# One 128-partition output store in place of two 64-partition stores, in a fused attention and MLP kernel

## The chip, the cores and the metric

The kernel runs on one core of a Trainium2 chip. The time is the device time of one execution in microseconds (us). Before the change it was 218.69 us, the median of 3 runs (217.29 to 221.75).

Engines, as the profile abbreviates them: PE is the matmul engine, PEld its weight loads, DVE VectorE, ACT ScalarE, POOL GpSimd, SP SyncE. "SPq" is SP's sequencer, which issues nearly all transfers, one after the other in the timelines below (its queue carries 96576 of the 96742 packets of the kernel before); the moving is done by DMA engines, of which the page counts 16. L404 is a line of that kernel's file; a changed kernel has its lines moved by one or two.

## The reference, cut to what matters

```python
# q, k, v: (4, 8, 768, 64) float32; lam: (8,); w_in: (512, 2048); w_out: (2048, 512)
for each block of 64 tokens:          # causal attention with decay, state carried over blocks
    out = (q k^T * Dmask) v + (q * lam_pow) kv_state
    kv_state = lam^64 * kv_state + (k * rev_pow)^T v
x = attention output as (3072 tokens, 512)
h = x @ w_in;  g = h * sigmoid(1.702 h);  out = g @ w_out      # (3072, 512) float32
```

## The kernel before

The kernel works in six waves of 512 tokens. Waves 0 and 1 take 256 tokens each of two sequences, waves 2 to 5 take 128 tokens each of all four. In waves 0 and 1 two neighbouring tokens share a partition when they are loaded. Their output columns therefore come out in the order (j, m), where the token is 2m + j: first the 64 even tokens of a tile, then the 64 odd ones. A tile of 128 tokens by 512 float32 (256 KB) was stored like this:

```python
def store(w, g, o, cols=slice(0, d_model)):
    if w < 2:
        r0 = (2 * w + g // 2) * S + (g % 2) * P
        dst = out[r0 : r0 + P, cols].rearrange("(m j) d -> j m d", j=2)
        for j in range(2):
            nc.sync.dma_start(out=dst[j], in_=o[hd(j), :])     # 64 partitions, every second row
    else:
        r0 = g * S + w * P
        nc.sync.dma_start(out=out[r0 : r0 + P, cols], in_=o)   # 128 partitions, consecutive rows
```

The same SP queue carries what the matmuls of the later waves need: the loads of k, q and v, and two kinds of transposing transfers.

```python
def p_cast(w, p):                       # waves 2 to 5, p = 0 to 3
    ...                                 # VectorE writes kqs from the loaded k and q
    nc.sync.dma_start_transpose(out=kq_of[w, p]..., in_=kqs...)   # PE's scores wait for this

def p_out(w, p):
    ...
    nc.scalar.copy(xs.rearrange("s b h d -> s h b d"), o)
    nc.sync.dma_start_transpose(out=xT(w)[:, p], in_=xs...)       # xs has two buffers

def u_x(w, bl, p):                      # waves 0 and 1: ScalarE writes xT itself
    nc.scalar.copy(xT(w)[:, p, 2 * bl : 2 * bl + 2, :], uo_ps.pop((w, bl, p))[:, :, 0:P])
```

## Time and profile before

| | kernel before |
|---|---|
| time, median of 3 runs | 218.69 us (217.29 to 221.75) |
| profiled execution | span 220.2 us (this execution took 221.89 us, slower than the three above) |
| PE busy | 209.7 us, 95% |
| PE's part of the chain that ended last | 81% |
| transfers under way, first half | 9 tenths of the DMA engines' time in most slices |

From the profile page of the kernel before. The first line gives the busy us, the share of the span and the instruction count of PE. The next three cut the span into 40 slices of 5.5 us: PE's granted clock in tenths, the busy share of the DMA engines in tenths, and the GB/s that they moved. The last is the queue that SP issues on: its packets, MB, and share of 16 engines' time.

```profile
PE 209.7 (95%) x1769; PEld 108.9 (49%) x1769; DVE 107.6 (49%) x235; ACT 87.9 (40%) x178; POOL 33.8 (15%) x66
PEclk9999999999999969999999999999999999999999
DMA  4999999997898999999969899577975132200112
GB/s 137 282 283 294 373 373 366 313 282 181 178 221 178 158 197 208 194 241 213 234 122 191 223 198 212 125 158 189 229 155 95 27 95 76 95 0 0 48 51 95
q1 hardware_dynamic: 96576, 39.86, 75.9%
```

PE is the limit. The chain of waits of the kernel before (start us, duration us, what) leaves PE twice after the start-up:

```profile
69.94 7.44 DMA kq<-kqs x2
77.37 0.05 issue
...
82.89 5.38 DMA xT<-xs
...
103.45 0.33 PE ps_s L413 x8
```

In that stretch the chain follows transposing transfers. The last line is the first score of wave 3. The timeline of SP's queue in the kernel before (start us, duration us, then what was issued):

```profile
62.54 7.29 SPq L496 DMA_DIRECT2D out_dram<-o_sb  x8
69.94 1.40 SPq L404 DMA_TRANSPOSE kq<-kqs  x1
71.43 1.18 SPq L496 DMA_DIRECT2D out_dram<-o_sb  x2
72.71 3.53 SPq L404 DMA_TRANSPOSE kq<-kqs  x2
```

Wave 0's eight half stores stand directly ahead of the first transpose, and wave 1's first pair between it and the second. The timeline of PE in the kernel before has in brackets how long PE was idle before a line, and for what:

```profile
73.15 0.40 PE L413 MATMUL ps_s<-kq 64*128 64x128 bf16 x8 [1.92 <-DMA kq<-kqs]
77.42 0.40 PE L413 MATMUL ps_s<-kq 64*128 64x128 bf16 x8 [1.80 <-DMA kq<-kqs]
```

So PE waits for these transposes, some 2 us each.

### The profile page before, as it was taken

How to read it: one execution, taken by the hardware profiler on the slowest of the kernel's cores; microseconds unless marked ns; L12 is line 12 of the kernel's file. 1: busy time of each engine (PE TensorE's matmuls, PEld its weight loads, DVE VectorE, ACT ScalarE, POOL GpSimd, SP SyncE). 2: the span in 40 equal slices, each digit the busy share in tenths (PEclk: the TensorE clock that was granted, in tenths of full speed). 3: DMA queues.
4: the chain of work that ended last, by engine and by line, in shares of the span. 5: the costliest groups of instructions: out<-in, count | busy, mean ns of one | idle time of the engine just before them, and what ended most of it. 6: DMA issues, size and time to landing. Idle time of an engine off the chain costs nothing.

```text
span 220.2 us, 4480 instructions
## 1 busy us (share of the span) xinstructions
PE 209.7 (95%) x1769; PEld 108.9 (49%) x1769; DVE 107.6 (49%) x235; ACT 87.9 (40%) x178; POOL 33.8 (15%) x66
## 2 busy tenths in 40 slices
PE   7989899999999499899999999999999999999994
PEld 2554344457854376444454444554444544444443
DVE  6686466572769748172664193572392532100121
ACT  5666661146612244246631056621076520366000
POOL 7593000373004000004000053000040000000000
PEclk9999999999999969999999999999999999999999
DMA  4999999997898999999969899577975132200112
GB/s 137 282 283 294 373 373 366 313 282 181 178 221 178 158 197 208 194 241 213 234 122 191 223 198 212 125 158 189 229 155 95 27 95 76 95 0 0 48 51 95
DMA packets 96742, 40.15 MB, mean 182 GB/s; under 512 B 77137, under 2 KB 89681, under 8 KB 96721
## 3 DMA queue, kind: packets, MB, share of 16 engines
q1 hardware_dynamic: 96576, 39.86, 75.9%
q8 instruction: 14, 0.23, 0.4%
q14 instruction: 8, 0.06, 0.1%
q10 hardware_dynamic: 144, 0.00, 0.0%
HBM read 27.27 MB, written 6.29 MB: 152 GB/s over the span
## 4 chain that ended last, share of the span: by engine, by line
PE 81%; DMA 11%; SPq 5%; DVE 1%; issue 0%; ACT 0%; ACTq 0%
PE ps_out L506 35%; PE ps_h L475 35%; SPq L89 4%; DMA kq<-kqs 3%; DMA ring<-in_moe_w_in_dram 3%; DMA xT<-xs 2%; PE ps_o L450 2%; PE ps_s L413 2%; DMA ring<-in_k_dram 2%; PE ps_out L521 2%; PE ps_o L443 1%; PE ps_kv L428 1%; PE ps_t L287 1%; PE ps_s L309 1%; SPq L117 1%; PE ps_o L382 1%
## 5 line engine op out<-in xcount | busy, mean ns | idle before, releaser
L475 PE MATMUL ps_h<-xT,w_in 128*128 128x512 bf16 (+1 forms) x448 | 88.5, 354 | 0.6 <-DVE w_in L150 0.6
L481 ACT ACTIVATE g_sb<-ps_h 128x512 bf16<-128x512 f32 (+1 forms) x112 | 59.1, 537 | 64.5 <-PE ps_h L475 63.7
L506 PE MATMUL ps_out<-w_out,g_sb 128*128 128x512 bf16 x368 | 83.4, 379 | 0.0
L475 PEld LDWEIGHTS <-w_in 128*128 128x128 bf16 x448 | 43.7, 100 | 39.8 <-DVE w_in L150 1.1
L506 PEld LDWEIGHTS <-g_sb 128*128 128x128 bf16 x368 | 34.7, 98 | 39.3
L513 DVE COPY o_sb<-ps_out 128x512 f32<-128x512 f32 x19 | 13.1, 691 | 53.6 <-PE ps_out L506 53.5
L420 DVE SCALAR_TENSOR_TENSOR sm<-ps_s,inv_pow,mask 128x512 bf16<-128x512 f32 x32 | 22.6, 747 | 28.0 <-PE ps_s L413 28.0
L453 ACT CAST xs<-ps_o 128x512 bf16<-128x512 f32 x16 | 9.4, 586 | 24.7 <-PE ps_o L450 21.8
L270 POOL TENSOR_TENSOR kqs<-ring,kq_pow 128x256 bf16<-128x256 f32 x16 | 10.3, 664 | 27.6 <-DMA ring<-in_q_dram 26.7
L402 POOL CAST v_bd<-ring 128x512 bf16<-128x512 f32 x8 | 4.9, 647 | 58.2 <-DMA ring<-in_v_dram 58.2
L402 POOL CAST v_sb<-ring 128x512 bf16<-128x512 f32 x8 | 7.2, 935 | 40.6 <-DMA ring<-in_v_dram 40.6
L314 DVE TENSOR_TENSOR sm<-ps_s,mask 128x512 bf16<-128x512 f32 x16 | 11.0, 684 | 2.7 <-PE ps_s L309 2.5
L432 DVE SCALAR_TENSOR_TENSOR kv<-kv,blk,ps_kv 64x256 bf16<-64x256 bf16 x24 | 11.4, 475 | 0.2
L400 DVE TENSOR_SCALAR kqs<-ring,q_pow 128x256 bf16<-128x256 f32 x32 | 11.2, 391 | 0.0
L400 DVE TENSOR_SCALAR kqs<-ring,k_pow 128x256 bf16<-128x256 f32 x32 | 10.5, 370 | 0.2
L262 PE MATMUL ps_f<-zeros 128*128 128x512 bf16 x25 | 9.2, 506 | 1.3 <-DVE zeros L180 1.3
L413 PE MATMUL ps_s<-kq 64*128 64x128 bf16 x128 | 6.4, 219 | 3.7 <-DMA kq<-kqs 3.7
L150 DVE CAST w_out<-ring 128x512 bf16<-128x512 f32 x16 | 7.2, 456 | 4.2 <-DMA ring<-in_moe_w_out_dram 4.2
L386 ACT CAST xT<-ps_o 128x256 bf16<-128x256 f32 x16 | 5.9, 371 | 8.3 <-DVE kv_bd L344 4.8
L270 DVE TENSOR_TENSOR kqs<-ring,kq_pow 128x256 bf16<-128x256 f32 x16 | 7.4, 482 | 3.0 <-DMA ring<-in_k_dram 2.3
L297 DVE COPY kq<-ps_t 128x512 bf16<-128x512 bf16 x10 | 4.2, 423 | 8.7 <-PE ps_t L287 8.7
L413 PEld LDWEIGHTS <-kq 64*128 64x128 bf16 x128 | 3.6, 94 | 9.8 <-issue 5.5
(68 smaller groups left out, 120.8 us busy)
## 6 DMA issues: line engine op xcount, KB each, us to landing
ring<-in_k_dram SPq DMA_DIRECT2D x23, 256.0 KB, 4.6
ring<-in_q_dram SPq DMA_DIRECT2D x23, 256.0 KB, 4.2
ring<-in_v_dram SPq DMA_DIRECT2D x23, 256.0 KB, 4.6
ring<-in_moe_w_in_dram SPq DMA_DIRECT2D x16, 256.0 KB, 6.4
ring<-in_moe_w_out_dram SPq DMA_DIRECT2D x16, 256.0 KB, 5.3
out_dram<-o_sb SPq DMA_DIRECT2D x15, 256.0 KB, 2.3
out_dram<-o_sb SPq DMA_DIRECT2D x16, 128.0 KB, 3.0
ring<-in_k_dram SPq DMA_DIRECT2D x2, 128.0 KB, 3.9
```

The source lines that it names most:

```text
L270: eng.tensor_tensor(kqs_of[w, p][:, bl, i].rearrange("s j h d -> s h j d"), read(w, "kq"[i], bl, p), tab, op=MUL)
L314: nc.vector.tensor_tensor(sm.rearrange("s h j t -> s h (j t)"), s_ps.pop((w, bl, p))[:, :, 0 : 2 * P], mask2.to_broadcast([P, 2, 2 * P]), ...
L400: nc.vector.tensor_scalar(kqs[:, i, :, h, :], x[:, :, p, h, :], scalar1=(k_pow, q_pow)[i][:, 2 * p + h : 2 * p + h + 1], scalar2=None, op0 ...
L402: nc.gpsimd.tensor_copy(v_sb[w % 2][:, p], read(w, "v")[:, :, p])
L413: nc.tensor.matmul(s[:, h, b, :], t[hd(h), 0, b, :], t[hd(h), 1, b, :], start=True, stop=True)
L420: nc.vector.scalar_tensor_tensor(sm[:, h], s[:, h], inv_pow[:, 2 * p + h : 2 * p + h + 1], mask.to_broadcast([P, B, P]), op0=MUL, op1=MUL)
L432: nc.vector.scalar_tensor_tensor(new[hd(h), p], old[hd(h), p], blk2[hd(h), p : p + 1], t[hd(h), :, hd(h)], op0=MUL, op1=ADD)
L453: nc.scalar.copy(xs.rearrange("s b h d -> s h b d"), o)
L475: nc.tensor.matmul(t[:, bs[0] * P : bs[1] * P], w_in_sb[fc // CW][:, kc, (fc % CW) * P : (fc % CW + 1) * P], xT(w)[:, kc, bs[0] : bs[1], : ...
L481: nc.scalar.activation(g_tile(w)[:, fc, c], h_ps.pop((w, fc))[:, c], GELU)
L506: nc.tensor.matmul(t, g_of[w][:, fc, g * P : (g + 1) * P], w_out_sb[j][:, fc % CW, :], start=(fc == 0), stop=(fc == FFC - 1))
L513: nc.vector.tensor_copy(o, t)
```

## The change

The intent is fewer and better transfers: eight stores in place of sixteen, each from all 128 partitions. There is support for it. In the trace's packet records the 2 KB packets of the half stores took about 160 ns each in the wave-0 burst, against 84 to 87 ns for whole-tile stores. Why the packets of a half store take longer is not shown.

```diff
         if w < 2:
             r0 = (2 * w + g // 2) * S + (g % 2) * P
-            dst = out[r0 : r0 + P, cols].rearrange("(m j) d -> j m d", j=2)
-            for j in range(2):
-                nc.sync.dma_start(out=dst[j], in_=o[hd(j), :])
+            nc.sync.dma_start(out=out[r0 : r0 + P, cols].rearrange("(m j) d -> j m d", j=2),
+                              in_=o)
```

In the built programs, as the author read them, one half store had the destination pattern 64 x 512 and the source 64 x 512. The new one has the destination 2 x 64 x 512 and the source 128 x 1 x 512. Nothing else in the order of the instructions changes.

## The prediction

> What bounds the kernel now. The page puts PE at 95% of a 220.2 us span and 81% of the chain that ended last on PE; the rest of that chain is loads until about 23 us and one stretch, from 69.9 to 88.3 us, where it runs through transfers of the stores' queue: "DMA kq<-kqs x2 7.44" from 69.94 and "DMA xT<-xs 5.38" from 82.89. In the timeline PE waits 1.92 us at 73.15 and 1.80 us at 77.42 for kq transposes. In the 40 slices the DMA engines are at 9 tenths through most of the first half.
>
> What the change intends. The sixteen 64-partition stores (128 KB) take a median 0.584 us each on the queue's sequencer, the whole stores of later waves 0.356 us, so eight fewer issues save 5 to 6 us of sequencer time. In the trace's packet records their 2 KB packets took about 160 ns each in the wave-0 burst, against 84 to 87 ns for whole-tile stores and weights: a tile costs each of 16 engines 8 x 160 = 1.3 us. A whole store over 16 engines would take 0.7 us. All that could shorten the stretch by 2 to 4 us at most.
>
> Why I expect the opposite. The new destination pattern, as the instruction carries it, is 2 x 64 x 512: its slowest dimension has size 2. [...] No transfer in the trace of before tests this.
>
> Cost, estimated from the trace's durations: each store puts 64 packets of 84 ns = 5.4 us on each of two engines, while 14 idle; before, 1.3 us on each of 16. What is behind it on the queue needs those two engines too, so the queue moves at their pace: +4.1 us per store, 33 us over eight.
>
> Critical share. The four wave-0 stores (from 62.5 us) are just ahead of the first kq transpose: it lands near 89 us in place of 73.1 (+16). One wave-1 store before the second transpose and one before the fourth add about 6 more by the xT transposes (+22 near 88 us). The last two (92.8, 96.3 us) stand before the wave-3 transposes, which have 1.2 us of slack (landing 102.2, used 103.45): +7. PE's long idle should cost another lowered-clock stretch, 1 to 3 us (the slice with PEclk 6 follows the waits of before). DVE's waits for o_sb buffers are mostly hidden. Sum about +30.
>
> Predicted: 249 us, 8 in 10 within 236 to 264. Faster by over 2%: 0.03, within 2%: 0.09, slower by over 2%: 0.88.
>
> What would show it. The stores' 1024 data packets stay, their completion packets fall from 16 x 16 to 8 x 2, so the page's 96742 becomes about 96502 (96614 if all 16 engines are used). Store landing goes from 3.0 us median to over 8. PE's wait for the first kq transpose grows from 1.9 to some 15 us or more; DMA busy falls to 2 to 5 tenths between 66 and 90 us. PE's busy work stays; after wave 3 starts the timelines run parallel.
>
> What would make it wrong: the transfer is spread over all 16 engines after all (then 215 to 219 us); a lone engine moves 2 KB packets at other than 84 ns; later slack absorbs the last two stores (then about 242).

Read "on each of two engines" there as the assumption: it rests on the leading 2 of the destination, and no transfer in the trace of the kernel before tests it. 16, 6 and 7 us and 1 to 3 us of lowered clock make the "about +30", and all of them stand on that assumption.

## More of the kernel before

Most runs fell in the ordinary ("fast") state. A run is marked slow when it is over 1.5% above the fastest of the same kernel.

## The result

The changed kernel took 248.56 us (median of 4 runs, 247.25 to 250.10), against 219.18 us (median of 4). The ratio was 1.1376, with a 95% interval of 1.1255 to 1.1496: slower. All ratios here are those for the fast runs, so they are not quite the ratios of the medians quoted beside them.

The same lines from the profile page of the changed kernel (span 248.4 us, slices of 6.2 us):

```profile
PE 214.3 (86%) x1769; PEld 110.8 (45%) x1769; DVE 108.5 (44%) x235; ACT 87.9 (35%) x178; POOL 31.8 (13%) x66
PEclk9999999999985579779976999999999999999999
DMA  5999999999319779996879899894699412310022
GB/s 155 303 319 309 391 371 312 256 211 219 85 51 71 85 134 76 175 223 144 99 117 180 141 194 228 173 241 95 159 230 201 88 39 74 105 42 0 0 87 84
q1 hardware_dynamic: 96336, 39.86, 75.7%
```

Three readings. The bytes are the same, but 240 packets are gone, all of them of 4 bytes (3264 on q1 before, 3024 after): 16 stores with 16 completions each became 8 stores with 2 each (256 - 16 = 240). I read that as one completion per engine, so that each new store ran on two DMA engines. The packet records bear it out: between 60 and 90 us two packets of 2 KB were under way together for 23.2 us and three for 2.5 us, where the kernel before had 14 to 16 together for 4.9 us. Second, from slice 11 on, for about 25 us, the traffic falls to 51 to 85 GB/s. That is the pace of two engines: the packet records of this stretch hold about 125 store packets of 2 KB in 5 us, which is 51 GB/s. Shared by two engines, that is one packet in 80 ns per engine. Third, PE's busy time grew by 4.6 us although it ran the same instructions; the granted clock fell to between 5 and 8 tenths in slices in and after the long waits.

The timeline of SP's queue in the changed kernel, the answer to the one above:

```profile
60.74 10.42 SPq L494 DMA_DIRECT2D out_dram<-o_sb  x4
71.27 9.97 SPq L404 DMA_TRANSPOSE kq<-kqs  x1
81.35 0.51 SPq L494 DMA_DIRECT2D out_dram<-o_sb  x1
81.97 8.41 SPq L404 DMA_TRANSPOSE kq<-kqs  x2
```

Four stores now take longer to issue than eight did, and the first transpose is held at its issue for 9.97 us in place of 1.40. The sequencer's own work is not the limit, since the same issue took 1.40 us before: by these times it is held while the stores ahead of it drain at 51 GB/s. PE's timeline of the changed kernel, only lines with a wait:

```profile
85.61 0.61 PE L413 MATMUL ps_s<-kq 64*128 64x128 bf16 x8 [14.61 <-DMA kq<-kqs]
91.67 0.40 PE L413 MATMUL ps_s<-kq 64*128 64x128 bf16 x8 [1.64 <-DMA kq<-kqs]
100.53 0.61 PE L413 MATMUL ps_s<-kq 64*128 64x128 bf16 x8 [2.85 <-DMA kq<-kqs]
106.77 0.38 PE L443 MATMUL ps_o<-kv,kq 64*128 64x64 bf16 x8 [2.11 <-ACT xs L453]
129.22 0.61 PE L413 MATMUL ps_s<-kq 64*128 64x128 bf16 x8 [6.39 <-DMA kq<-kqs]
```

The two profiled executions differ by 28.2 us. Two milestones divide it: the first wave-2 score (73.15 before, 85.61 after) and the first wave-3 score (103.45 before, 129.22 after).

| stretch | before us | after us | difference |
|---|---|---|---|
| start to first wave-2 score | 73.15 | 85.61 | 12.5 |
| from there to first wave-3 score | 30.30 | 43.61 | 13.3 |
| from there to the end | 116.75 | 119.18 | 2.4 |

The profiled execution of the kernel before was a late one: SP reached its wave-0 stores at 62.54 us, against 60.74 in the changed kernel and 60.06 to 60.40 in k16r, natural and natural_two below. So the first row is too small by nearly 2 us, which fits the 30.2 us that the ratio gives for the whole (0.1376 x 219.18) against the 28.2 here.

### The profile page after: what moved, and what is told of

It is laid out like the page before. It is cut to its first block, busy times and chain, and to the rows that moved or that the text cites. A ratio compares the mean times of both kernels' runs of the same rounds, so it can differ in the third digit from the quotient of the medians.

```text
span 248.4 us, 4470 instructions
## 1 busy us (share of the span) xinstructions
PE 214.3 (86%) x1769; PEld 110.8 (45%) x1769; DVE 108.5 (44%) x235; ACT 87.9 (35%) x178; POOL 31.8 (13%) x66
## 2 busy tenths in 40 slices
DMA packets 96501, 40.15 MB, mean 162 GB/s; under 512 B 76896, under 2 KB 89440, under 8 KB 96480
## 4 chain that ended last, share of the span: by engine, by line
PE 61%; DMA 29%; SPq 6%; DVE 1%; issue 1%; ACT 1%; ACTq 0%; DVEq 0%
PE ps_h L475 26%; PE ps_out L505 26%; DMA kq<-kqs 12%; DMA ring<-in_moe_w_out_dram 7%; DMA out_dram<-o_sb 3%; SPq L89 3%; DMA ring<-in_moe_w_in_dram 3%; DMA xT<-xs 2%; DMA ring<-in_v_dram 2%; PE ps_o L450 2%; PE ps_s L413 2%; SPq L101 2%; PE ps_out L520 1%; SPq L117 1%; PE ps_kv L428 1%; PE ps_o L443 1%
## 5 line engine op out<-in xcount | busy, mean ns | idle before, releaser
L475 PE MATMUL ps_h<-xT,w_in 128*128 128x512 bf16 (+1 forms) x448 | 90.2, 359 | 0.6 <-DVE o_sb L512 0.6
L505 PE MATMUL ps_out<-w_out,g_sb 128*128 128x512 bf16 x368 | 85.4, 386 | 0.4 <-DVE w_out L150 0.4
L475 PEld LDWEIGHTS <-w_in 128*128 128x128 bf16 x448 | 44.3, 101 | 40.9 <-issue 3.2
L505 PEld LDWEIGHTS <-g_sb 128*128 128x128 bf16 x368 | 35.3, 100 | 40.7 <-issue 2.6
L413 PE MATMUL ps_s<-kq 64*128 64x128 bf16 x128 | 7.0, 235 | 25.5 <-DMA kq<-kqs 25.5
L400 DVE TENSOR_SCALAR kqs<-ring,q_pow 128x256 bf16<-128x256 f32 x32 | 11.8, 411 | 0.0
L400 DVE TENSOR_SCALAR kqs<-ring,k_pow 128x256 bf16<-128x256 f32 x32 | 11.5, 401 | 0.2
L432 DVE SCALAR_TENSOR_TENSOR kv<-kv,blk,ps_kv 64x256 bf16<-64x256 bf16 x24 | 11.4, 475 | 0.2
L402 POOL CAST v_sb<-ring 128x512 bf16<-128x512 f32 x8 | 5.1, 680 | 45.9 <-DMA ring<-in_v_dram 45.9
L262 PE MATMUL ps_f<-zeros 128*128 128x512 bf16 x25 | 8.1, 456 | 1.3 <-DVE zeros L180 1.3
```

Source lines behind the costliest of these rows:

```text
L400: nc.vector.tensor_scalar(kqs[:, i, :, h, :], x[:, :, p, h, :], scalar1=(k_pow, q_pow)[i][:, 2 * p + h : 2 * p + h + 1], scalar2=None, op0 ...
L402: nc.gpsimd.tensor_copy(v_sb[w % 2][:, p], read(w, "v")[:, :, p])
L413: nc.tensor.matmul(s[:, h, b, :], t[hd(h), 0, b, :], t[hd(h), 1, b, :], start=True, stop=True)
L432: nc.vector.scalar_tensor_tensor(new[hd(h), p], old[hd(h), p], blk2[hd(h), p : p + 1], t[hd(h), :, hd(h)], op0=MUL, op1=ADD)
L475: nc.tensor.matmul(t[:, bs[0] * P : bs[1] * P], w_in_sb[fc // CW][:, kc, (fc % CW) * P : (fc % CW + 1) * P], xT(w)[:, kc, bs[0] : bs[1], : ...
L505: nc.tensor.matmul(t, g_of[w][:, fc, g * P : (g + 1) * P], w_out_sb[j][:, fc % CW, :], start=(fc == 0), stop=(fc == FFC - 1))
```

## The experiments

The theory (S, for spread): the only cause is that the leading destination dimension of 2 puts a store on two of the 16 DMA engines, and everything behind it on the queue goes at their pace. The rivals: M, one 256 KB transfer with interleaved rows ahead of the transposes is what delays them; Q, eight fewer transfers shift which completion each later issue waits for.

To vary the leading dimension, and by theory S the number of engines with it, the experiments permute the 128 output columns of a tile. If the columns are in the order (r, m), where the token is R m + r, then one store of the whole tile has the destination R x (128/R) x 512. The permutation is made in the ScalarE copy that writes xT. It costs no extra instruction, and every result was correct.

### two_k2: two engines, but nothing merged

```diff
+            dst = out[r0 : r0 + P, cols].rearrange("(m r) d -> r m d", r=4)
+            for j in range(2):
+                nc.sync.dma_start(out=dst[2 * j : 2 * j + 2], in_=o[hd(j), :])
 # u_x: xT written as "s x (r j m) -> s x j m r", read as "s x (j m r) -> s x j m r"
```

> Theory S (spread): the slowdown comes only from the leading destination dimension of 2, which puts a store on 2 of 16 DMA engines. Rival M: it comes from merging, i.e. one 256 KB store from 128 partitions to interleaved rows ahead of the transposes. Rival Q: from eight fewer transfers, which shifts the completion semaphores that later issues wait on. This kernel merges nothing: 16 stores of 64 partitions as before, but the output columns are permuted so that each store's destination is 2 x 32 x 512 (leading dimension 2, 32 packets on each of two engines, two such stores per tile). S expects 245 to 252 us and 3041 completion packets in all minus none, i.e. stores with 2 completions each (96,517 packets on the page, 240 minus 16 fewer than before); M and Q expect 217 to 222 us and 96,742 packets.

It took 251.3 us (249.78 to 252.97; before 218.97; ratio 1.1483, interval 1.1415 to 1.1551), with 96517 packets as S expected. It is as slow as the change, with sixteen stores of 64 partitions. One thing was not as intended: the permuted ScalarE copy took 1.31 us in place of 0.37, so a cleaner run had to follow.

### k16: merged and interleaved, but 16 engines

```diff
-            nc.sync.dma_start(out=out[r0 : r0 + P, cols].rearrange("(m j) d -> j m d", j=2),
+            nc.sync.dma_start(out=out[r0 : r0 + P, cols].rearrange("(m r) d -> r m d", r=16),
                               in_=o)
 # u_x: xT written as "s x (r j m) -> s x j m r", with r=8
```

> One store of 128 partitions per tile, as in the change, 8 transfers in all, destination rows interleaved even wider (16 x 8 x 512, rows 32 KB apart), but the leading dimension is 16. S expects 214 to 219 us, 96,614 packets, and the first kq transposes landing no later than in the kernel before. M and Q expect about the time of the changed kernel, 245 us or more.

It took 225.59 us (ratio 1.0253, interval 1.0167 to 1.0339): far from 248, but outside what S expected. The groups by shape show a likely reason, which k16r below confirms. The lines are of the kernel before and of k16; after the bar stand busy us and mean ns of one:

```profile
L386 ACT CAST xT<-ps_o 128x256 bf16<-128x256 f32 x16 | 5.9, 371 | 8.3 <-DVE kv_bd L344 4.8 <-PE ps_o L382 3.4
```

```profile
L386 ACT CAST xT<-ps_o 128x256 bf16<-128x256 f32 x16 | 20.0, 1247 | 6.6 <-DVE kv_bd L344 4.0 <-PE ps_o L382 2.3
```

Writing 2-byte elements at steps of 32 bytes took 3.4 times as long as writing them side by side. The experiment had added a cost of its own, on an engine that feeds PE.

### natural and natural_two: what the merging is worth when it is done well

In both, the columns are put into plain token order, so that a tile is 128 consecutive rows. natural stores it by one transfer, natural_two by two of 64 partitions.

```diff
-        nc.scalar.copy(xT(w)[:, p, 2 * bl : 2 * bl + 2, :], uo_ps.pop((w, bl, p))[:, :, 0:P])
+        nc.scalar.copy(xT(w)[:, p, 2 * bl : 2 * bl + 2, :].rearrange("s x (m j) -> s x j m", j=2),
+                       uo_ps.pop((w, bl, p))[:, :, 0:P].rearrange("s x (j m) -> s x j m", j=2))
 ...
+            nc.sync.dma_start(out=out[r0 : r0 + P, cols], in_=o)                    # natural
 ...
+            for j in range(2):                                                       # natural_two
+                nc.sync.dma_start(out=out[r0 + 64 * j : r0 + 64 * j + 64, cols], in_=o[hd(j), :])
```

> The columns of waves 0 and 1 are put into token order in the ScalarE copy that makes xT, so that a store is 128 consecutive rows of 2 KB, one whole contiguous 256 KB transfer over 16 engines. S expects 213 to 218 us: the stores take 0.36 us to issue in place of two of 0.58, their packets 84 ns in place of 160, so the first kq transpose lands 2 to 3 us earlier; gain 1 to 4 us over the kernel before unless the strided ScalarE write (372 ns before) slows much. M expects about 245 us, Q too.

> Same token order as the run natural, but each tile still stored by two transfers of 64 partitions (contiguous rows). It separates the price of two half stores from the permuted copy. Expected: packets near 160 ns again in the wave-0 burst, time as before, 217 to 220 us, that is 1 to 3 us above natural, if merging over 16 engines is worth what I put it at; no difference if merging is worth nothing.

natural took 219.21 us (ratio 1.0019, interval 0.9972 to 1.0067), natural_two 219.41 us (1.0016, interval 0.9968 to 1.0064); the kernel before had 218.97 us. The packet times were as expected, 84 ns in natural's wave-0 burst and about 160 ns in natural_two's. The time did not follow: natural's gain of 1 to 4 us was a miss, and the two came out the same, the case that I had named for a merging that is worth nothing. Here the permuted copy took 0.45 us (steps of 4 bytes). k16r, below, has no such cost and shows no gain either, so the copy does not hide one.

### k16r, k8r, k4r, two_k2r: the number of engines as the only thing that changes

The permutation moves to the reading side of the ScalarE copy, so that it writes side by side, and the copy takes its old 0.37 us again.

```diff
-        nc.scalar.copy(xT(w)[:, p, 2 * bl : 2 * bl + 2, :], uo_ps.pop((w, bl, p))[:, :, 0:P])
+        nc.scalar.copy(xT(w)[:, p, 2 * bl : 2 * bl + 2, :].rearrange("s x (r j m) -> s x r j m", j=2, r=R // 2),
+                       uo_ps.pop((w, bl, p))[:, :, 0:P].rearrange("s x (j m r) -> s x r j m", j=2, r=R // 2))
 ...
+            nc.sync.dma_start(out=out[r0 : r0 + P, cols].rearrange("(m r) d -> r m d", r=R), in_=o)
 # R = 16, 8 or 4; two_k2r has R = 4 and the two half stores of two_k2
```

> The run k16 was confounded: its permuted ScalarE copy took 1.25 us in place of 0.37. Here the permutation is on the reading side of that copy (contiguous writes), everything else as in k16: one store per tile, destination 16 x 8 x 512. If S (spread) is right and the copy is cheap again: 216 to 220 us, no more than natural; merging as such (M) or fewer transfers (Q) as the cause would give about 248.

> One store per tile to a destination of 8 x 16 x 512: by S 8 engines with 16 packets of 84 ns, 1.34 us per store, what a tile cost each engine before (1.3 us). S expects 217 to 221 us and 8 completion packets fewer per store than at 16 engines (96,549 or 96,550 in all). M and Q expect about 248.

> Destination 4 x 32 x 512: by S 4 engines with 32 packets, 2.7 us per store. Four stores from about 64.5 us end near 75.5, the first kq transpose lands 3 to 4 us later than before, the second and the wave-3 ones add 1 to 2 each: 222 to 228 us, so clearly between 8 engines and 2 (248.6). Packets about 96,518. M and Q expect about 248 for all of these.

> The run two_k2 again with the cheap form of the permuted copy: sixteen stores of 64 partitions, each on two engines by its 2 x 32 x 512 destination, no merging. S expects the time of the changed kernel, 246 to 251 us, M and Q that of the kernel before, 217 to 221.

The numbers of completions follow from the packets: the kernel before had 96742 on its page, with 256 completions of these stores. A page can differ by one packet of another queue (q14 has 8 on the page of the kernel before and 7 on that of the changed one).

| kernel | stores | leading dimension | completions by the packets | time, us | ratio, 95% interval |
|---|---|---|---|---|---|
| before | 16 of 64 partitions | 64 | 16 each | 219.10 | |
| k16r | 8 of 128 | 16 | 16 each (96613) | 219.08 | 1.0022, 0.9948 to 1.0095 |
| k8r | 8 of 128 | 8 | 8 each (96549) | 221.75 | 1.0081, 0.9993 to 1.0170 |
| k4r | 8 of 128 | 4 | 4 each (96517) | 233.78 | 1.0660, 1.0591 to 1.0728 |
| two_k2r | 16 of 64 | 2 | 2 each (96517) | 253.52 | 1.1562, 1.1486 to 1.1638 |
| the change (its own rounds) | 8 of 128 | 2 | 2 each (96501) | 248.56 | 1.1376, 1.1255 to 1.1496 |

This settles it between the three. k16r and k8r have everything that M and Q blame (one transfer of 128 partitions, interleaved rows, eight fewer transfers) and cost at most a little. two_k2r merges nothing, has sixteen transfers, and is slow. The time goes with the leading dimension. The medians of k8r and k4r include one slow run each; the ratios do not. k4r's profile was that slow run, so nothing of it is used but the packet count.

Two sizes missed what I expected. k4r was to cost 3 to 9 us and cost 14.5 (0.066 x 219.1). Per store it puts 2.7 us on an engine (estimated, 32 packets of 84 ns), where the kernel before put 1.3 (8 of 160 ns), so by the queue's pace alone the estimate is 11 us over eight stores. There is no slack that hides it, and the rest is not explained: part may be the lower clock (0.956 to 0.971 in k4r's fast runs, 0.992 to 1.0 in the kernel before), but no run tests that. And two_k2r came out 5 us slower than the change, with the same packets by count on the same number of engines. The two ran in different rounds and their intervals just overlap, so this difference is not certain. PE's waits in two_k2r, next to those of the change shown above:

```profile
87.49 0.61 PE L414 MATMUL ps_s<-kq 64*128 64x128 bf16 x8 [14.59 <-DMA kq<-kqs]
93.64 0.55 PE L414 MATMUL ps_s<-kq 64*128 64x128 bf16 x8 [2.37 <-DMA kq<-kqs]
133.42 0.61 PE L414 MATMUL ps_s<-kq 64*128 64x128 bf16 x8 [7.73 <-DMA kq<-kqs]
```

The waits are the same ones, each milestone 2 to 4 us later. Of the first 2 us, 1.2 are a later arrival at the stores (61.91 against 60.74 us). Whether two transfers of 32 packets per engine are really worse than one of 64, and why, was not tested and stays open.

Why is there nothing to win with 16 engines? The SP timeline of k16r:

```profile
60.25 3.63 SPq L495 DMA_DIRECT2D out_dram<-o_sb  x4
67.66 1.33 SPq L405 DMA_TRANSPOSE kq<-kqs  x1
```

and two lines of its SP waits (us in total, times, longest us):

```profile
SPq L405 <- PE ps_h L476: 9.3, 9, 1.9
SPq L405 <- DVE kqs L401: 6.8, 6, 3.7
```

The stores are issued by 63.88 us, and then the queue stands until 67.66, because the transpose needs what VectorE is still casting (its longest wait for that is 3.7 us). In the kernel before the transpose was issued at 69.94, right behind the stores, but its profiled run had reached them 2.3 us later, which is the whole difference. The fair pair is natural_two and natural, which reach the stores within 0.4 us of each other. Their SP timelines, natural_two first:

```profile
60.06 6.43 SPq L496 DMA_DIRECT2D out_dram<-o_sb  x8
67.29 1.35 SPq L405 DMA_TRANSPOSE kq<-kqs  x1
```

```profile
60.40 2.73 SPq L495 DMA_DIRECT2D out_dram<-o_sb  x4
68.16 1.33 SPq L405 DMA_TRANSPOSE kq<-kqs  x1
```

The whole stores are issued 3.4 us sooner (63.13 against 66.49), and the transpose goes out no sooner: natural's longest wait for the cast is 5.0 us, natural_two's 0.8. The faster stores only give back their time as a wait for the cast.

### only_w0 and only_w1: the two terms of the sum, apart

```diff
+            if w == 0:          # only_w1: w == 1
+                nc.sync.dma_start(out=dst, in_=o)
+            else:
+                for j in range(2):
+                    nc.sync.dma_start(out=dst[j], in_=o[hd(j), :])
```

> Only wave 0's four tiles are stored by the new transfer, wave 1's by two transfers as before. By the sum in the prediction the four wave-0 stores carry +16 us (in the changed kernel the first kq transpose was used 12.5 us later than before), and little of it should be lost later: 231 to 237 us. PE's wait for the first kq transpose about 12 to 15 us, the one before wave 3 gone.

> Only wave 1's four tiles are stored by the new transfer. By the sum: 6 us from the first two, 7 us from the last two, which stand before the wave-3 transposes: 229 to 235 us; PE's wait for the first kq transpose as before (under 3 us), a wait of 5 us or more before wave 3. With only_w0 the two excesses should add up to about the 29.5 us of the whole change if the queue's pace is all there is.

only_w0 took 231.64 us (ratio 1.0516, interval 1.0429 to 1.0602), only_w1 235.80 us (1.0737, interval 1.0668 to 1.0806), the kernel before 220.23 us. In us that is 11.4 and 16.2 (the ratio less one, times 220.23), together 27.6, against 30.2 for the whole change (0.1376 x 219.18). The parts add up nearly. only_w1 is just above the 229 to 235 us that I expected, and its 16.2 us are more than the 13 of the sum. The waits are where they should be. PE's timeline has in only_w0 one long wait, and none before wave 3; in only_w1 the second and the wave-3 transposes are waited for, and the first is not. The lines of only_w0, then of only_w1:

```profile
86.75 0.61 PE L413 MATMUL ps_s<-kq 64*128 64x128 bf16 x8 [14.62 <-DMA kq<-kqs]
```

```profile
78.56 0.61 PE L413 MATMUL ps_s<-kq 64*128 64x128 bf16 x8 [6.06 <-DMA kq<-kqs]
115.13 0.61 PE L413 MATMUL ps_s<-kq 64*128 64x128 bf16 x8 [7.48 <-DMA kq<-kqs]
```

In only_w0 the first wave-2 score comes 13.6 us later than before (86.75 against 73.15), but the span is only 10.4 us longer: 3.2 us come back, about what PE waited for the next transposes in the kernel before (1.80 us at 77.42, and 1.17 at 89.01 for an xT transpose), which have now arrived.

### act_queue: the stores on ScalarE's own queue

```diff
-            nc.sync.dma_start(out=out[r0 : r0 + P, cols].rearrange("(m j) d -> j m d", j=2),
+            nc.scalar.dma_start(out=out[r0 : r0 + P, cols].rearrange("(m j) d -> j m d", j=2),
                               in_=o)
```

> The eight two-engine stores are issued from ScalarE's own DMA queue in place of the shared one. The work on the two engines is the same, but the transposes no longer stand behind the stores in one queue. If the order in the queue is what makes the 5.4 us per store visible: 222 to 238 us, the first kq transpose landing well before 85 us (the issues also come earlier, about 43 us on, and take ScalarE time, so some loss stays). If only the amount of work on the two engines counts: 245 us or more.

It took 252.39 us (ratio 1.1481, interval 1.1411 to 1.1551). My expectation was wrong: a second queue does not help. The page of act_queue isolates the stores, because q10 carries little else (144 packets in the kernel before): 1040 more packets are 1024 of data and 16 completions, so two per store again. Its chain of waits shows where the time went instead.

```profile
q10 hardware_dynamic: 1184, 2.10, 2.3%
```

```profile
48.00 18.62 DMA ring<-in_k_dram
66.63 0.02 issue
66.65 0.02 ACTq L494
...
87.06 11.45 DMA kq<-kqs
```

The stores now go out from 45 us on, and the loads beside them crawl: the chain follows one load of k for 18.62 us, and the page's traffic falls from 269 to 90 GB/s at 50 us. How an engine divides its time between two queues was not shown. ScalarE also stood still from 59.5 to 66.65 us before it could issue its fourth store. So the run shows that the two engines' work was not hidden by another queue at this place (252.39 us, against 248.56 for the change). It does not show that work on them costs the same at any place. Moving the eight stores to the last wave, where the page shows the DMA engines at 0 to 2 tenths (its last four slices), would have tested that.

### warm: dummy matmuls while PE waits

```diff
     def p_score(w, p):
         t = kq_of[w, p]
+        fill({(2, 0): 55, (3, 0): 22}.get((w, p), 0))
```

> The changed kernel with 55 dummy matmuls (128 x 512, 0.22 us each) ahead of the wave-2 scores and 22 ahead of the wave-3 scores, where PE otherwise waits 14.6 and 6.4 us for a transpose. It asks what part of the loss is the lower granted clock after PE's idling (half clock in some 31 us of the trace; PE's busy time 4.6 us more than before). If that part is real time: granted clock back near 0.99, 2 to 5 us faster than the changed kernel, 243.5 to 246.5 us. If the half-clock stretches fall where the queue sets the pace anyway: no gain, 248 to 249 us.

It took 246.82 us (ratio 1.1247, interval 1.1162 to 1.1331). Its interval overlaps that of the change, which ran in other rounds, so by the times alone it is not clear. It also fell between the two outcomes that I had named (243.5 to 246.5, and 248 to 249). The traces say more. The windows view gives the granted clock (the number before the DMA share and the GB/s) in the disturbed stretch and after it. First the changed kernel, then warm:

```profile
62.00:125.00 63.00, 39.04 (x336) 22.12 (x334) 25.16 (x61) 15.38 (x33) 4.83 (x8) 0.81 0.88 114
125.00:149.00 24.00, 19.78 (x174) 10.00 (x175) 10.49 (x18) 5.92 (x10) 0.00 (x0) 0.86 0.92 161
```

```profile
62.00:125.00 63.00, 55.22 (x408) 29.18 (x413) 25.59 (x62) 15.56 (x33) 4.69 (x8) 0.92 0.81 115
125.00:147.00 22.00, 18.56 (x178) 9.55 (x179) 10.49 (x18) 5.92 (x10) 0.00 (x0) 1.00 1.09 184
```

With the clock kept up after wave 3 starts, the time from there to the end is 116.9 us (245.5 less 128.64), as in the kernel before (116.75), where the change has 119.2. Before that point nearly nothing is gained: the transposes land when they land. So the lower clock is worth some 2 to 3 us of the loss by these two profiles, and the rest is waiting. The clock records of the changed kernel hold four stretches at half clock, 30.7 us together; the longest, 17.1 us from 72.7 us on, begins in PE's first long wait (71.0 to 85.6 us). The kernel before has one of 3.4 us from 78.6 us on. That idling lowers the clock, the changed kernel and warm show together: 0.81 in the disturbed stretch, and 0.92 once dummy matmuls fill part of the waits.

## Why the prediction was right, point by point

The time was 248.56 us, predicted 249, inside the range. What held and what did not:

- **Two engines per store: right.** The packets on the stores' queue fell by 240, to the packet as computed, and stores with leading dimensions of 16, 8, 4 and 2 had 16, 8, 4 and 2 completions each. Other dimensions, and the part of the source pattern, were not tested.
- **5.4 us per store and engine: a little high.** 64 packets of 84 ns. The stretch moved one in 80 ns, so 5.1 us.
- **First transpose +16 us: too high.** It moved PE's first wave-2 score by 12.5 us. Of the 3.5 us, 1.8 are the profiled run's earlier arrival at the stores (60.74 against 62.54) and about 1 the packet time; the rest was not traced. In only_w0, the four stores of wave 0 cost 11.4 us in the end.
- **+22 by the xT transposes and +7 more for wave 3, 13 after the first transpose: right in sum.** The traces show +17.8 (106.77 against 89.01, read from the chain of the kernel before) and another 8.0 up to wave 3, so 13.3 after the first transpose. But only_w1 shows 16.2 us for wave 1's stores alone. So the mechanism was right, but that the total came out within 1 us is partly luck: two errors cancel, a wave-0 term that was too large (16 us, where only_w0 cost 11.4) and a wave-1 term that was too small (13, where only_w1 cost 16.2).
- **Lowered clock, 1 to 3 us: about right.** 2.4 us after wave 3 starts, and warm takes them away.
- **"DMA busy falls to 2 to 5 tenths": only half right.** The row of busy tenths shows 3 and 1, and then 9 and 7, while the GB/s stay at 51 to 85. A packet seems to count as busy while it waits: in the 5 us from 75 us on, 469 packets of transposes took 124 us together, 263 ns on average, with a median of 18 ns; 20 of them took over 5 us each. For starved engines read the GB/s.
- **"Store landing over 8 us": could not be read.** The page's landing times take a transfer's sixteenth completion, and these have two. The page of the changed kernel gives 2.0 us for stores, which is that of the later waves alone.
- **What the change could have gained, 2 to 4 us at most: there was nothing.** k16r and natural give the same time as before; in their traces the first transpose waits for VectorE's cast (up to 3.7 and 5.0 us).

No version beat the kernel before.

## What to carry to other kernels

Before merging transfers, write down the destination pattern that the merged transfer will carry, and look at its slowest dimension: here 2 x 64 x 512 put a store on two DMA engines (2 completions, 51 GB/s), and the transpose behind the stores was held at its issue for 9.97 us in place of 1.40. If the tokens come out in an awkward order, permute them in a copy that is made anyway, so that the outermost dimension is not small: with 16 the time was as before (219.08 us), with 8, 4 and 2 it was 221.75, 233.78 and 248.56 us. Watch that this copy still writes side by side: for 128 x 256 elements of 2 bytes it took 0.37 us so, 0.45 at steps of 4 bytes, 1.25 at 32 bytes and 1.31 at 128 bytes. And before speeding up a transfer, look at what the next thing on the queue waits for: twice the speed of the stores (packets of 84 ns in place of about 160) was worth nothing here (219.21 and 219.41 us), because a cast was late.
